# Attention and a feed-forward block on one core: probabilities copied by transfers and transposed as float32r, with another order of the work in a slot

## The chip, the core and the metric

The kernel runs on one core of one Trainium2 chip. The metric is the device time of one execution in microseconds (us). Five engines work side by side, each through its own instructions in the order in which they were written: TensorE (PE in the profile, its weight loads PEld), VectorE (DVE), ScalarE (ACT), GpSimd (POOL) and SyncE (SP), whose queue issues all transfers here. They wait for one another by semaphores.

## The reference, cut to what matters

```python
# q, k, v: 8 batches x 8 heads x 576 x 64; f: 8 x 8 x 576
scores = q @ k.T / 8 + (cum[:, None] - cum[None, :])     # cum = cumsum(log(clip(f)))
scores = where(causal, -1e9, scores)
attn = softmax(scores)                                   # row maximum taken off, sum + 1e-9
x = heads of (attn @ v) side by side                     # 8 x 576 x 512
xn = (x - mean(x)) / sqrt(var(x) + 1e-6) * g_ln
out = x + relu(xn @ w_ch1) @ w_ch2                       # 512 -> 2048 -> 512
```

The precision wanted is that of float32. TensorE multiplies float32r operands quicker than float32 ones but with fewer bits, so most operands are kept as a high part (float32r) and a low part (the rest, float32r too), and a product is made of two or three matmuls.

## The kernel before, in words

There are 64 heads (n). A head's 576 queries are cut into tiles of 64, 128, 128, 128 and 128 rows (t = 0 to 4), and tile t needs only the keys up to its own. The work is a row of *slots*, one for each head and t = 1 to 4; t = 0 rides along with t = 1. Heads 0 to 15 ("full") work in float32 while the weights are being prepared; heads 16 to 63, the *later heads*, work with high and low parts.

In a slot, pieces named by letters are recorded in the order that a string of ORDERS gives. From slot 66 on (the later heads but for the first two slots and a bit) one string holds to the end. The pieces:

- Q: scores of this slot's tile, `s` (lines L373 and L374: two matmuls, from `hi` and from `kl` and `xq`). S: mask and row maximum on VectorE, from `s` into the softmax tile `p` (L406). e: exponential and row sum on ScalarE, in place (L417). B: reciprocal of the sum on VectorE (L422, L423), normalisation on GpSimd (L424).
- t: transposes on TensorE, `tr` from `p`, of the tile of two slots ago (LAG = 2), 128 columns at a time (L430): 3, 3, 4 and 5 of them for t = 1 to 4. h: ScalarE copies `tr` into the high part `ph` (L486). l: VectorE writes the low parts into `ph` and `pl` (L491).
- A: probabilities times values, `o` from `ph`, `pl` and `vv` (L525), in the slots t = 1 and t = 3, each for two tiles, the later of which was transposed in the slot before. F and a: the result goes by way of `ot` into `xs` (L561, L572) and from there to memory.
- M: the first feed-forward matmul, twelve of 256 columns into `h` (L604 to L606). r: ScalarE makes its high part (L612). m: VectorE makes the low part (L617). N: the second one for the step before, six of 512 columns into `acc` (L626 to L628).
- R: loads (`xr`) and splitting (`x`) of tokens for the next chunk of 256 tokens; near a chunk's end the chunk's rows are loaded (`xw`) and, two slots later, transposed (`xp`, L430 too), copied by ScalarE (`xt`, L651) and their mean and variance taken by VectorE (`bs`, L656). After a chunk's last N two VectorE instructions (L685) form the output. A chunk takes 16 feed-forward steps, one a slot: four heads.
- P: preparation of the next head: ScalarE casts `raw` into `hi` (L339 in slot t = 2, L345 in t = 3), GpSimd makes the low parts, VectorE `xq` and `vv`; also the load of `raw` for the head after that. L: a few small GpSimd instructions.

All tiles come from pools with a fixed number of buffers (`p` has three), so that a write waits for the last reader of its buffer. The transposes take `p` as float32 with `ident`, the identity's float32 view.

Of the kernel before, what the change touches and what calls it, by code (L numbers as in the profile page):

```python
# [8 lines left out]
F32 = mybir.dt.float32  # L9
F32R = mybir.dt.float32r  # L10
# [16 lines left out]
NFULL = 16  # L27
# [20 lines left out]

ORDERS = [
    (0, "WwQsSthAeMrgFBmlLNPaRf"),  # L50
    (37, "WwQSstAMhPelgNFrfmBLRa"),
    (66, "AthQFlMSPNreamRBL"),
]


# [1 line left out]
def attn_moe(ctx: ExitStack, tc: tile.TileContext, qk, v, f, g, w1, w2, out):  # L57
    nc = tc.nc

    const = ctx.enter_context(tc.tile_pool(name="const", bufs=1))  # L60
    work = ctx.enter_context(tc.tile_pool(name="work", bufs=1))
# [5 lines left out]
    pools = {}  # L67
# [14 lines left out]
    ident = identr.bitcast(F32)  # L82

    def busy(n):
# [9 lines left out]
        out=mask[:, S - P :], in_=mask[:, S - P :], pattern=[[-1, P]], base=0,  # L94
# [42 lines left out]
    class WPrep:  # L137
# [131 lines left out]
        late = None  # L269
# [32 lines left out]
    def new_xq(name, dt):  # L302
        xq = work.tile([66, S], dt, tag="xq", bufs=2, name=name)
        nc.gpsimd.memset(xq[64:66, :].bitcast(F32), 1.0)
        return xq

    def load(n):
        h = Head()
        h.n, h.full = n, n < NFULL
        if h.full:  # L310
            h.kl = work.tile([66, S], F32, tag="kl", bufs=2, name=f"kl{n}")
            if len(xfs) < 2:
                xfs.append(new_xq(f"xf{n}", F32))
            h.xq = xfs[n % 2]
            nc.sync.dma_start(out=h.xq[0:64, :], in_=qk[n][0:64, 0, :])
            nc.sync.dma_start(out=h.kl[0:64, :], in_=qk[n][0:64, 1, :])
            if n > 0:
                nc.sync.dma_start(out=h.kl[64:66, :], in_=cumd[n])
        else:
            h.raw = pools["late"].tile([P, 2, S], F32, tag="raw", bufs=1, name=f"raw{n}")  # L320
            nc.sync.dma_start(out=h.raw, in_=qk[n])
# [9 lines left out]
    def prep_a(h):  # L331
        n = h.n
        h.hi = pools["late"].tile([P, 2, S], F32R, tag="hi", bufs=2, name=f"hi{n}")
        h.kl = work.tile([66, S], F32R, tag="kl", bufs=2, name=f"kl{n}")
        if len(xqs) < 2:
            xqs.append(new_xq(f"xq{len(xqs)}", F32R))
        h.xq = xqs[(n - NFULL) % 2]
        nc.sync.dma_start(out=h.kl[64:66, :].bitcast(F32), in_=cumd[n])
        nc.scalar.copy(out=h.hi[:, 1, :], in_=h.raw[:, 1, :])  # L339
        nc.gpsimd.tensor_tensor(  # L340
            out=h.kl[0:64, :], in0=h.raw[0:64, 1, :], in1=h.hi[0:64, 1, :].bitcast(F32), op=ALU.subtract
        )

    def prep_b(h):
        nc.scalar.copy(out=h.hi[:, 0, :], in_=h.raw[:, 0, :])  # L345
        nc.vector.tensor_copy(out=h.xq[0:64, :], in_=h.raw[0:64, 0, :])
        nc.gpsimd.tensor_tensor(
            out=h.hi[64:128, 0, :], in0=h.raw[64:128, 0, :], in1=h.hi[64:128, 0, :].bitcast(F32), op=ALU.subtract
        )

    def prep_v(h):
# [24 lines left out]
                z, sp = a + QT[0][2], sp[: QT[0][1], : QT[0][2]]  # L376
            h.s[t].append((a, z, sp))

    corners, padded = [], {}

    def padded_keys(tag, width, zeros):
        if tag not in padded:
# [36 lines left out]
    def softmax_b(h, t):  # L419
        q0, m, w = QT[t]  # L420
        pt, st = h.p[t]
        nc.vector.tensor_scalar_add(st[:m, 3:4], st[:m, 2:3], 1e-9)  # L422
        nc.vector.reciprocal(st[:m, 3:4], st[:m, 3:4])  # L423
        nc.gpsimd.tensor_scalar(  # L424
            out=pt[:m, :w], in0=pt[:m, :w], scalar1=st[:m, 3:4], scalar2=1.0, op0=ALU.mult, op1=ALU.mult
        )

    def tr(out_, in_):
        m = in_.shape[0]
        nc.tensor.transpose(out_, in_, ident[:m, :m])  # L430

# [196 lines left out]
    def tokens(c, k, t0, m, out_):  # L630

        t = t0
        while t < t0 + m:
            b, o = divmod(t, S)
            src, o0, lim = (xd1[b], 0, S1) if o < S1 else (xd2[b], S1, S)
            w = min(t0 + m - t, lim - o)
            nc.sync.dma_start(out=out_[:, t - t0 : t - t0 + w], in_=src[P * k : P * k + P, o - o0 : o - o0 + w])
            t += w

    def rows_load(c, i):  # L640
        c.xw = m2(f"xw{c.n}_{i}", F32).rearrange("p (k c) -> p k c", k=KT)
        for k in range(KT):
            tokens(c, k, c.n * C + P * i, P, c.xw[:, k, :])

    def chunk_rows(c, i):

# [128 lines left out]
    for u, slot in enumerate(slots):  # L775

        def before(k):
            return slots[u - k] if u >= k else None

        if slot is not None:  # L780
            n, t = slot
            h = hd[n]
        av = None
        if before(LAG + 1) is not None and before(LAG + 1)[1] in (2, 4):
            av = hd[before(LAG + 1)[0]]
        want = moe.can(wp.ready()) and u >= FIRST_MOE

        def piece(c):
            tu = before(LAG)
            if c == "t" and tu is not None:  # L790
                transpose_unit(hd[tu[0]], tu[1])
            elif c == "h" and tu is not None:
                transposed_hi(hd[tu[0]], tu[1])
            elif c == "l" and tu is not None:
                transposed_lo(hd[tu[0]])
            elif c == "Q" and slot is not None:
                if t == 1:
                    qk_mm(h, 0)
                qk_mm(h, t)
            elif c == "A" and av is not None:  # L800
                av_unit(av, before(LAG + 1)[1])
            elif c == "S" and slot is not None:
                if t == 1:
                    softmax_a(h, 0)
                softmax_a(h, t)
            elif c == "e" and slot is not None:
                if t == 1:
                    softmax_e(h, 0)
                softmax_e(h, t)
            elif c in FILL:  # L810
                wp.fill(FILL[c])
            elif c == "s":
                wp.sums()
                if u == LAG:
                    busy(WARM[2])
            elif c == "F" and av is not None:
                finish(av)
            elif c == "a" and av is not None:
                finish_add(av)
            elif c == "r" and want:  # L820
                moe.first_high()
            elif c == "R":
                moe.limit = min(NCHUNK, max(0, u - LAG - 1) // (4 * H) * S // C)
                moe.rest()
            elif c == "L":
                run_later(RSTD)
            elif c == "M" and want:
                moe.first()
            elif c == "B" and slot is not None:
                if t == 1:  # L830
                    softmax_b(h, 0)
                softmax_b(h, t)
            elif c == "m" and want:
                moe.first_low()
            elif c == "W":
                due = 1 + min(u, W_CHANGE) / W_SLOTS + max(0, u - W_CHANGE) * W_TICKS
                while not wp.done() and wp.tick_no <= due:
                    wp.tick()
            elif c == "N":
                moe.second()  # L840
            elif c == "P":
                prep()

        def prep():

            if slot is not None:
                if t == 1 and n + 1 < NFULL:
                    start_head(n + 1)
                if n == NFULL - 2 and t == 1:
                    while not wp.done():  # L850
                        wp.tick()
                        wp.fill(99)
                    early.close()
                    pools["late"] = ctx.enter_context(tc.tile_pool(name="late", bufs=1))
                if n + 1 >= NFULL and n + 1 < B * H:
                    if t == 2:
                        prep_a(hd[n + 1])
                    if t == 3:
                        prep_b(hd[n + 1])
                if t == 3 and n + 2 >= NFULL and n + 2 < B * H:  # L860
                    start_head(n + 2)
                if not h.full and t == LAG + 1:
                    prep_v(h)
                if t == LAG + 1 and n + 1 < B * H:
                    load_v(hd[n + 1])

        for c in [o for first, o in ORDERS if first <= u][-1]:
            piece(c)
# [47 lines left out]
```

## Time and profile before

| | |
|---|---|
| median of 3 runs (lowest to highest) | 1228.06 us (1227.03 to 1229.16) |
| the profiled execution's own time | 1236.05 us |
| its span in the profile | 1234.3 us |
| busy share of the span: PE, PEld, DVE, ACT, POOL | 98%, 88%, 62%, 52%, 36% |
| transfers | 98.82 MB in q1, 26.5% of 16 engines |

In the profile a row of a timeline gives start, duration, engine, line, operation, output and inputs, and in square brackets the idle time before it and what ended that. A row by form gives the count, the busy time, the mean duration in ns of one, and the idle time before. Matmuls are pipelined, so that their records overlap: what one costs is read from the starts of neighbours. In a window's row the width comes first, then the busy time of PE, PEld, DVE, ACT and POOL with their counts, the granted clock of TensorE, the transfers' share and GB/s.

### The profile page before, as it was taken

Reading aid. Unit: us, or ns where it says so; the run is one execution under the profiler, and the core shown is the slowest. Engines: PE = TensorE matmul, PEld = TensorE weight load, DVE = VectorE, ACT = ScalarE, POOL = GpSimd, SP = SyncE. Lnnn points to the kernel's source line nnn. Section 1 sums busy time; section 2 is a strip of 40 time slices with the busy share of each in tenths; the row PEclk is TensorE's granted clock in tenths of the full one; section 3 lists DMA queues with packets and bytes.
Section 4 is the critical chain, followed back from the end, with each engine's and each line's share of the span. In section 5 each row is a group of like instructions: output and inputs, shape, how many; then the busy total and the mean of one; then the engine's idle time right before and its main releaser. Section 6 shows DMA issues by size and latency. Waiting matters only on the chain.

```text
span 1234.3 us, 25357 instructions
## 1 busy us (share of the span) xinstructions
PE 1210.6 (98%) x8368; PEld 1088.0 (88%) x8368; DVE 762.5 (62%) x2664; ACT 643.4 (52%) x1936; POOL 445.1 (36%) x767
## 2 busy tenths in 40 slices
PE   8888998999999999999999999999999999999998
PEld 6666887899999999999999999999999999999997
DVE  6777684477776767777767676767777762222222
ACT  5887574555655555555555555556555542112111
POOL 3444343444444435343434344444444320000000
PEclk8998998999999999999999999999999999999999
DMA  6454351222223232322222222222222311110100
GB/s 174 138 169 143 117 157 57 76 68 79 81 77 94 77 94 77 89 78 84 71 73 90 81 90 81 73 89 82 79 64 76 95 37 36 51 35 26 44 26 27
DMA packets 91253, 100.45 MB, mean 81 GB/s; under 512 B 26865, under 2 KB 76017, under 8 KB 91121
## 3 DMA queue, kind: packets, MB, share of 16 engines
q1 hardware_dynamic: 91120, 98.82, 26.5%
q8 instruction: 67, 1.10, 0.4%
q14 instruction: 66, 0.53, 0.1%
HBM read 79.61 MB, written 19.17 MB: 80 GB/s over the span
## 4 chain that ended last, share of the span: by engine, by line
PE 93%; DVE 3%; ACT 2%; DMA 1%; POOL 1%; issue 1%; DVEq 0%; SPq 0%; ACTq 0%; POOLq 0%
PE h L604 11%; PE h L605 11%; PE h L606 11%; PE acc L626 11%; PE acc L627 11%; PE acc L628 11%; PE tr L430 8%; PE o L525 6%; PE s L373 3%; PE s L374 3%; PE s L371 3%; PE o L500 2%; PE xp L430 1%; PE pc L201 1%; DVE p L406 1%; ACT p L417 1%
## 5 line engine op out<-in xcount | busy, mean ns | idle before, releaser
L424 POOL TENSOR_SCALAR p<-p,st 64x64 f32<-64x64 f32 (+4 forms) x320 | 168.9, 532 | 454.6 <-DVE st L423 161.2
L604 PE MATMUL h<-x,w1h 128*128 128x256 f32 x1152 | 329.3, 286 | 0.4 <-DVE st L406 0.4
L605 PE MATMUL h<-x,w1h 128*128 128x256 f32 x1152 | 325.4, 282 | 0.0
L606 PE MATMUL h<-x,w1l 128*128 128x256 f32 x1152 | 325.4, 282 | 0.0
L612 ACT ACTIVATE hh<-h 128x256 fp32r<-128x256 f32 x288 | 110.7, 384 | 308.7 <-PE h L606 308.4
L617 DVE SCALAR_TENSOR_TENSOR hh<-h,hh 128x256 fp32r<-128x256 f32 x288 | 121.1, 420 | 186.0 <-ACT hh L612 179.8
L626 PE MATMUL acc<-w2h,hh 128*128 128x512 f32 x576 | 228.2, 396 | 0.0
L627 PE MATMUL acc<-w2l,hh 128*128 128x512 f32 x576 | 227.6, 395 | 0.0
L628 PE MATMUL acc<-w2h,hh 128*128 128x512 f32 x576 | 224.7, 390 | 0.0
L604 PEld LDWEIGHTS h<-x,w1h 128*128 128x128 f32 x1152 | 219.2, 190 | 6.1 <-issue 0.9
L605 PEld LDWEIGHTS h<-x,w1h 128*128 128x128 f32 x1152 | 219.7, 191 | 3.3
L606 PEld LDWEIGHTS h<-x,w1l 128*128 128x128 f32 x1152 | 219.4, 190 | 0.0
L417 ACT ACTIVATE p<-p,st 64x64 f32<-64x64 f32 (+4 forms) x320 | 178.3, 558 | 60.3 <-DVE st L406 58.4
L486 ACT CAST ph<-tr 64x128 fp32r<-64x128 f32 (+4 forms) x384 | 109.2, 333 | 124.6 <-PE tr L430 107.1
L430 PE MATMUL tr<-identr,p 128*128 128x128 f32 (+1 forms) x896 | 143.1, 276 | 8.9 <-POOL p L424 6.8
L430 PEld LDWEIGHTS tr<-identr,p 128*128 128x128 f32 (+1 forms) x896 | 101.0, 131 | 38.9 <-POOL p L424 18.2
L406 DVE CUSTOM_DVE_ANT_0 p<-s,mask 64x64 f32<-64x64 f32 (+4 forms) x320 | 130.2, 419 | 7.1 <-PE s L371 3.5
L628 PEld LDWEIGHTS acc<-w2h,hh 128*128 128x128 f32 x576 | 108.3, 188 | 24.8
L491 DVE TENSOR_TENSOR ph<-tr,ph 64x192 fp32r<-64x192 f32 x192 | 57.8, 301 | 115.2 <-ACT ph L486 112.3
L626 PEld LDWEIGHTS acc<-w2h,hh 128*128 128x128 f32 x576 | 109.4, 190 | 14.1 <-issue 0.2
L627 PEld LDWEIGHTS acc<-w2l,hh 128*128 128x128 f32 x576 | 109.3, 190 | 11.8
L373 PE MATMUL s<-hi 128*128 128x288 f32 (+4 forms) x288 | 96.2, 355 | 0.0
(84 smaller groups left out, 1828.0 us busy)
## 6 DMA issues: line engine op xcount, KB each, us to landing
raw<-in_qk_dram SPq DMA_DIRECT2D x48, 576.0 KB
wr<-in_w_dram SPq DMA_DIRECT2D x32, 512.0 KB
vr<-in_v_dram SPq DMA_DIRECT2D x64, 160.0 KB
out_dram<-xt SPq DMA_DIRECT2D x36, 256.0 KB
xa<-xs SPq DMA_DIRECT2D x32, 160.0 KB
xb<-xs SPq DMA_DIRECT2D x32, 128.0 KB
xw<-xa SPq DMA_DIRECT2D x64, 64.0 KB
xw<-xb SPq DMA_DIRECT2D x48, 64.0 KB
```

The lines of the kernel that those rows point to most:

```text
L373: mm(sp, h.hi[:, 0, q0 : q0 + m], h.hi[:, 1, a:z], start=True, stop=False)
L406: nc.vector.tensor_tensor_reduce(out=pt[:m, a:z], in0=sp, in1=mask[:m, off + a : off + z], scale=-SCALE, scalar=3.0e38 if i == 0 else st[: ...
L417: nc.scalar.activation(pt[:m, :w], pt[:m, :w], AF.Exp, bias=st[:m, i : i + 1], scale=-1.0, accum_out=st[:m, 2:3])
L424: nc.gpsimd.tensor_scalar(out=pt[:m, :w], in0=pt[:m, :w], scalar1=st[:m, 3:4], scalar2=1.0, op0=ALU.mult, op1=ALU.mult)
L430: nc.tensor.transpose(out_, in_, ident[:m, :m])
L604: mm(ph, w1h[:, k, fs], c.x[k][:, 0, :], start=(k == 0), stop=False)
L605: mm(ph, w1h[:, k, fs], c.x[k][:, 1, :], start=False, stop=False)
L606: mm(ph, w1l[:, k, fs], c.x[k][:, 0, :], start=False, stop=(k == KT - 1))
L617: nc.vector.scalar_tensor_tensor(out=h[:, 1, :], in0=ph, scalar=0.0, in1=h[:, 0, :].bitcast(F32), op0=ALU.max, op1=ALU.subtract)
L626: mm(c.acc[i], h[:, 0, ts_], w2h[:, j, :], start=(j == 0), stop=False)
L627: mm(c.acc[i], h[:, 0, ts_], w2l[:, j, :], start=False, stop=False)
L628: mm(c.acc[i], h[:, 1, ts_], w2h[:, j, :], start=False, stop=(j == FT - 1))
```

## The change

For later heads, piece B issues one more thing: a transfer copies the normalised `p` into a tile `pw` of type float32r (for t = 0 a small one, `pw0`, made once; for even t a tile of its own with one buffer; for odd t one of the three buffers of `p`). The transposes read `pw` with the identity as float32r and write their output as float32r. The chunk's rows `xw` are loaded into a float32r tile too, by the same transfers as before, and transposed as such. `raw` becomes two tiles, one for the keys and one for the queries, each with a load of its own, in a new piece D at the end of the slots t = 2 and t = 3. And the string for the slots from 66 on is another.

```diff
 ORDERS = [
     (0, "WwQsSthAeMrgFBmlLNPaRf"),
-    (37, "WwQSstAMhPelgNFrfmBLRa"),
-    (66, "AthQFlMSPNreamRBL"),
+    (37, "WwQSstAMhPelgNFrfmBDLRa"),
+    (66, "QSAFeMaBPrthNmlRLD"),
 ]
...
+    def load_raw(h, i):
+        h.raw[i] = pools["late"].tile([P, S], F32, tag=f"raw{i}", bufs=1, name=f"raw{h.n}_{i}")
+        nc.sync.dma_start(out=h.raw[i], in_=qk[h.n][:, i, :])
...
         nc.gpsimd.tensor_scalar(
             out=pt[:m, :w], in0=pt[:m, :w], scalar1=st[:m, 3:4], scalar2=1.0, op0=ALU.mult, op1=ALU.mult
         )
+        if not h.full:
+            if t == 0:
+                if not words:
+                    words.append(pools["late"].tile([P, D], F32R, tag="pw0", bufs=1, name="pw0"))
+                    nc.gpsimd.memset(words[0].bitcast(F32), 0.0)
+                pw = words[0]
+            elif t % 2 == 0:
+                pw = pools["late"].tile([P, S], F32R, tag="pw", bufs=1, name=f"pw{h.n}_{t}")
+            else:
+                pw = work.tile([P, S], F32R, tag="p", bufs=3, name=f"pw{h.n}_{t}")
+            nc.sync.dma_start(out=pw[:m, :w].bitcast(F32), in_=pt[:m, :w])
+            h.p[t] = (pw, st)

     def tr(out_, in_):
         m = in_.shape[0]
-        nc.tensor.transpose(out_, in_, ident[:m, :m])
+        if in_.dtype == F32R:
+            nc.tensor.transpose(out_.bitcast(F32R), in_, identr[:m, :m])
+        else:
+            nc.tensor.transpose(out_, in_, ident[:m, :m])
...
     def rows_load(c, i):
-        c.xw = m2(f"xw{c.n}_{i}", F32).rearrange("p (k c) -> p k c", k=KT)
+        c.xw = m2(f"xw{c.n}_{i}", F32R).rearrange("p (k c) -> p k c", k=KT)
         for k in range(KT):
-            tokens(c, k, c.n * C + P * i, P, c.xw[:, k, :])
+            tokens(c, k, c.n * C + P * i, P, c.xw[:, k, :].bitcast(F32))
```

How the instructions stand then. TensorE, head 49, slot t = 1 (names carry the head, the tile and a buffer number); before:

```order
L525 MATMUL o48_2_10776<-ph1_48_10673,vv48_10709 128x320
L525 MATMUL o48_2_10776<-ph1_48_10673,vv48_10709 128x256
L525 MATMUL o48_2_10776<-ph1_48_10673,vv48_10709 128x128
L525 MATMUL o48_2_10776<-pl1_48_10674,vv48_10709 64x256
L525 MATMUL o48_2_10776<-pl1_48_10674,vv48_10709 64x128
L430 MATMUL tr48_3_10784<-identr_71,p48_3_10701 64x128
L430 MATMUL tr48_3_10784<-identr_71,p48_3_10701 128x128 x3
L373 MATMUL s49_0_0_10791<-hi49_10645 64x128
L374 MATMUL s49_0_0_10791<-kl49_10646,xq1_2930 64x128
L373 MATMUL s49_1_0_10794<-hi49_10645 128x192
L374 MATMUL s49_1_0_10794<-kl49_10646,xq1_2930 128x192
L604 MATMUL h9_8_10802<-x9_0_9876,w1h_135 128x256
```

and after:

```order
L376 MATMUL s49_0_0_11145<-hi49_10999 64x128
L377 MATMUL s49_0_0_11145<-kl49_11000,xq1_2939 64x128
L376 MATMUL s49_1_0_11148<-hi49_10999 128x192
L377 MATMUL s49_1_0_11148<-kl49_11000,xq1_2939 128x192
L543 MATMUL o48_2_11156<-ph1_48_11077,vv48_11070 128x320
L543 MATMUL o48_2_11156<-ph1_48_11077,vv48_11070 128x256
L543 MATMUL o48_2_11156<-ph1_48_11077,vv48_11070 128x128
L543 MATMUL o48_2_11156<-pl1_48_11078,vv48_11070 64x256
L543 MATMUL o48_2_11156<-pl1_48_11078,vv48_11070 64x128
L622 MATMUL h9_8_11167<-x9_0_10210,w1h_135 128x256
```

The scores moved ahead of A, and the transposes behind M's twelve matmuls: `tr48_3` now stands between the last L624 and the first L644 (N), and reads `pw48_3`.

VectorE from slot t = 3 to t = 4 of head 49, where a chunk's rows are transposed in t = 3 (`bs`, `sv` are their statistics, `st` the softmax sums, ISA is S); before:

```order
L617 SCALAR_TENSOR_TENSOR hh9_10_10963<-h9_10_10931,hh9_10_10963 128x256
L656 BN_STATS bs9_0_10977<-xt9_0_10973 128x6
L657 BN_AGGR sv9_10975<-bs9_0_10977 128x2
L422 TENSOR_SCALAR st49_3_10945<-st49_3_10945 128x1
L423 RECIPROCAL st49_3_10945<-st49_3_10945 128x1
L491 TENSOR_TENSOR ph1_49_10915<-tr49_2_10991,ph1_49_10915 64x128
L491 TENSOR_TENSOR pl1_49_10916<-tr49_2_10991,ph1_49_10915 128x256
L406 ISA p49_4_11018,st49_4_11019<-s49_4_0_10997,mask_129 128x288
L406 ISA st49_4_11019 128x1
```

and after:

```order
L674 BN_STATS bs9_0_11356<-xt9_0_11352 128x6
L675 BN_AGGR sv9_11354<-bs9_0_11356 128x2
L409 ISA p49_4_11375,st49_4_11376<-s49_4_0_11369,mask_129 128x288
L409 ISA st49_4_11376 128x1
L409 ISA p49_4_11375,st49_4_11376<-s49_4_1_11372,mask_129,st49_4_11376 128x288
L409 ISA st49_4_11376 128x1
L425 TENSOR_SCALAR st49_4_11376<-st49_4_11376 128x1
L426 RECIPROCAL st49_4_11376<-st49_4_11376 128x1
L635 SCALAR_TENSOR_TENSOR hh9_11_11398<-h9_11_11380,hh9_11_11398 128x256
L509 TENSOR_TENSOR ph1_49_11330<-tr49_2_11400,ph1_49_11330 64x128
L509 TENSOR_TENSOR pl1_49_11331<-tr49_2_11400,ph1_49_11330 128x256
```

Before, the low part of `tr49_2` came ahead of the slot's S; now S, the sums and m stand between the statistics and that low part, which A reads in the next slot. ScalarE at the same place, after (L420 is e, L630 r, L504 h, L669 the copy of the chunk's rows):

```order
L669 COPY xt9_0_11352<-xp9_0_11347 128x512
L420 ACTIVATE p49_4_11375,st49_4_11376<-p49_4_11375,st49_4_11376 128x576
L630 ACTIVATE hh9_11_11398<-h9_11_11380 128x256
L504 CAST ph1_49_11330<-tr49_2_11400 64x128
L504 CAST ph1_49_11330<-tr49_2_11400 128x256
```

Before, h of `tr49_2` stood right behind the copy `xt9_0`, and r and e behind it.

VectorE at a chunk's end, from slot t = 1 to t = 2 of head 51; before:

```order
L685 SCALAR_TENSOR_TENSOR xt9_1_11096<-acc9_1_10427,rs9_10976,xt9_1_11096 128x512
L572 TENSOR_TENSOR xs50_0_11308<-o50_2_11287,ot50_0_11309 64x320
L617 SCALAR_TENSOR_TENSOR hh10_0_11341<-h10_0_11313,hh10_0_11341 128x256
L422 TENSOR_SCALAR st51_0_11326<-st51_0_11326 64x1
L423 RECIPROCAL st51_0_11326<-st51_0_11326 64x1
L422 TENSOR_SCALAR st51_1_11329<-st51_1_11329 128x1
L423 RECIPROCAL st51_1_11329<-st51_1_11329 128x1
L491 TENSOR_TENSOR ph2_50_11293<-tr50_4_11353,ph2_50_11293 64x128
```

and after:

```order
L703 SCALAR_TENSOR_TENSOR xt9_1_11485<-acc9_1_10782,rs9_11355,xt9_1_11485 128x512
L635 SCALAR_TENSOR_TENSOR hh10_0_11723<-h10_0_11700,hh10_0_11723 128x256
L509 TENSOR_TENSOR ph2_50_11725<-tr50_3_11727,ph2_50_11725 64x128
L509 TENSOR_TENSOR pl2_50_11726<-tr50_3_11727,ph2_50_11725 128x3x128
L409 ISA p51_2_11750,st51_2_11751<-s51_2_0_11747,mask_129 128x320
L409 ISA st51_2_11751 128x1
L425 TENSOR_SCALAR st51_2_11751<-st51_2_11751 128x1
L426 RECIPROCAL st51_2_11751<-st51_2_11751 128x1
L635 SCALAR_TENSOR_TENSOR hh10_1_11777<-h10_1_11754,hh10_1_11777 128x256
L509 TENSOR_TENSOR ph2_50_11725<-tr50_4_11779,ph2_50_11725 64x128
```

The low part of `tr50_4`, wanted by A in slot t = 3, moved from right behind the chunk's end to behind two low parts more, S, the sums and the next m.

More of the change, by code (lines that the diff above doesn't have):

```diff
@@ L319, in load @@
         else:
-            h.raw = pools["late"].tile([P, 2, S], F32, tag="raw", bufs=1, name=f"raw{n}")
-            nc.sync.dma_start(out=h.raw, in_=qk[n])
-        return h
+            h.raw = {}
+        return h
+    def load_raw(h, i):
+        h.raw[i] = pools["late"].tile([P, S], F32, tag=f"raw{i}", bufs=1, name=f"raw{h.n}_{i}")
+        nc.sync.dma_start(out=h.raw[i], in_=qk[h.n][:, i, :])
     def load_v(h):
@@ L338, in prep_a @@
         nc.sync.dma_start(out=h.kl[64:66, :].bitcast(F32), in_=cumd[n])
-        nc.scalar.copy(out=h.hi[:, 1, :], in_=h.raw[:, 1, :])
+        nc.scalar.copy(out=h.hi[:, 1, :], in_=h.raw[1])
         nc.gpsimd.tensor_tensor(
-            out=h.kl[0:64, :], in0=h.raw[0:64, 1, :], in1=h.hi[0:64, 1, :].bitcast(F32), op=ALU.subtract
+            out=h.kl[0:64, :], in0=h.raw[1][0:64, :], in1=h.hi[0:64, 1, :].bitcast(F32), op=ALU.subtract
         )
     def prep_b(h):
-        nc.scalar.copy(out=h.hi[:, 0, :], in_=h.raw[:, 0, :])
-        nc.vector.tensor_copy(out=h.xq[0:64, :], in_=h.raw[0:64, 0, :])
+        nc.scalar.copy(out=h.hi[:, 0, :], in_=h.raw[0])
+        nc.vector.tensor_copy(out=h.xq[0:64, :], in_=h.raw[0][0:64, :])
         nc.gpsimd.tensor_tensor(
-            out=h.hi[64:128, 0, :], in0=h.raw[64:128, 0, :], in1=h.hi[64:128, 0, :].bitcast(F32), op=ALU.subtract
+            out=h.hi[64:128, 0, :], in0=h.raw[0][64:128, :], in1=h.hi[64:128, 0, :].bitcast(F32), op=ALU.subtract
         )
@@ L377, in qk_mm @@
             h.s[t].append((a, z, sp))
-    corners, padded = [], {}
+    corners, padded, words = [], {}, []
     def padded_keys(tag, width, zeros):
@@ L842, in piece, with next_raw @@
                 prep()
+            elif c == "D":
+                next_raw()
+        def next_raw():
+            if slot is not None and t in (2, 3) and NFULL <= n + 2 < B * H:
+                if t == 2:
+                    start_head(n + 2)
+                load_raw(hd[n + 2], 1 if t == 2 else 0)
         def prep():
@@ L859, in prep @@
                         prep_b(hd[n + 1])
-                if t == 3 and n + 2 >= NFULL and n + 2 < B * H:
-                    start_head(n + 2)
                 if not h.full and t == LAG + 1:
```

## The prediction

> **What bounds the kernel now.** I read the page's head, then the later heads' stretch as a window, then the waits of TensorE there.
>
> ```profile
> span 1234.3 us, 25357 instructions
> PE 1210.6 (98%) x8368; PEld 1088.0 (88%) x8368; DVE 762.5 (62%) x2664; ACT 643.4 (52%) x1936; POOL 445.1 (36%) x767
> ```
> ```profile
> 250.00:1000.00 750.00, 749.87 (x5313) 693.79 (x5312) 537.48 (x1919) 434.60 (x1315) 327.13 (x538) 1.00 0.26 81
> ```
> ```profile
> PEld xp L430 <- issue: 0.3, 1, 0.3
> ```
>
> From 250 to 1000 us TensorE (first number behind the width) is busy 749.87 of 750 us at full granted clock (1.00), and its waits are one of 0.3 us. So this stretch lasts as long as its matmuls follow one another; what shortens or holds TensorE's row there moves the end, nothing else does. The profiled execution took 1236.05 us (span 1234.3 and 1.75 around it), 8 us over the median of the runs, 1228.06; I work out a difference and put it on the median.
>
> **What an instruction costs in TensorE's row** is read from the starts of neighbours (records overlap, so durations say nothing):
>
> ```profile
> 501.31 0.28 PE L604 MATMUL h<-x,w1h 128*128 128x256 f32 x1
> ...
> 502.74 0.40 PE L626 MATMUL acc<-w2h,hh 128*128 128x512 f32 x1
> ...
> 504.13 0.49 PE L525 MATMUL o<-ph,vv 128*128 128x320 f32 x3
> 504.45 0.34 PE L525 MATMUL o<-pl,vv 128*64 128x256 f32 x2
> 504.62 0.60 PE L430 MATMUL tr<-identr,p 128*64 128x128 f32 x4
> ...
> 505.12 0.23 PE L374 MATMUL s<-kl,xq 66*64 66x128 f32 x1
> 505.18 0.31 PE L373 MATMUL s<-hi 128*128 128x192 f32 x1
> 505.33 0.27 PE L374 MATMUL s<-kl,xq 66*128 66x192 f32 x1
> 505.44 0.30 PE L604 MATMUL h<-x,w1h 128*128 128x256 f32 x1
> ```
> ```profile
> 508.28 0.60 PE L430 MATMUL tr<-identr,p 128*64 128x128 f32 x4
> 508.71 0.27 PE L430 MATMUL tr_4b<-identr,p 128*128 128x128 f32 x1
> ```
> ```profile
> L430 PEld LDWEIGHTS tr<-identr,p 128*128 128x128 f32 x576 | 72.2, 142 | 11.9 <-issue 1.3
> L430 PEld LDWEIGHTS tr<-identr,p 128*64 128x64 f32 x320 | 33.0, 112 | 27.1 <-POOL p L424 18.2 <-issue 4.2 <-POOL kl L340 0.3
> L373 PEld LDWEIGHTS s<-hi 128*128 128x128 f32 x240 | 45.6, 190 | 0.0
> L373 PEld LDWEIGHTS s<-hi 128*64 128x64 f32 x48 | 6.6, 137 | 0.0
> ```
>
> - Four float32 transposes (508.28 to 508.71) take 0.108 each, for 128 moving columns.
> - A float32r matmul of 128 moving columns takes 0.06 (505.12 to 505.18). 320+256+128 columns take 0.32 (504.13 to 504.45): 0.455 ns a column.
> - 192 columns should so take 0.087, but 505.33 to 505.44 is 0.11: there the load of the next 128 weight columns sets the pace. Two loads of `hi` differ by 53 ns for 64 columns, so 128 take about 0.107. The float32 transposes' loads differ by only 30 ns for 64.
> - M (12 matmuls, 501.31 to 502.74) takes 1.43, N (six, to 504.13) 1.39.
>
> **The change, part by part.**
>
> *Transposes as float32r.* No row shows one. From below: nothing gained, 0.108, if load or array go as before. From above: 0.06, the float32r matmul's. I take 0.06: 0.108 is two passes of 128 columns at 0.455 ns, the float32r matmul needs one, and the load in transpose mode is already the faster of the two. A gain of 0.048 counts only between transposes of a group: the last is followed by an ordinary load of 128 columns, which needs 0.11 anyway. Groups of 3, 3, 4 and 5 a head leave 11 gaps, 48 later heads 528; the tokens' 36 groups of four (`xp`) 108. 636 x 0.048 = 30.5 us less.
>
> *The new order on TensorE* removes no instruction. But A, which ended before a 64-column transpose (its last 128 moving columns cost 0.06), now ends before M's 128-column load: 0.11. Twice a head, 96 x 0.05 = 4.8 us more. Q then stands behind N's 512 columns, which hide its load.
>
> *The copies.* 240 copies p to pw and 48 more loads (raw split in two) go through SP's queue. An issue there takes 0.33, so six more a head are 2.0 us, on a queue that computes nothing.
>
> ```profile
> 516.87 0.33 SPq L321 DMA_DIRECT2D raw<-in_qk_dram  x1
> ```
> ```profile
> 88.59 3.36 DMA kl<-in_qk_dram
> ```
> ```profile
> 9.45 4.88 DMA wr<-in_w_dram
> ```
>
> Each copy waits for GpSimd's normalisation; behind it in SP's queue wait raw (read four slots later), xr and xw (one and two slots later) and vr. The largest copy has 288 KB, between kl's 144 KB (3.36 us) and wr's 512 KB (4.88). It is issued some 0.7 us into the slot after its own, and its transpose stands behind Q and M of the slot after that: an estimate of 5.1 us, from the slots' lengths worked out below. I take the lower row (both ends of a copy are on the core) and cost it at nothing; the cover is that slot between. The Trainium skill (DMA: Bandwidth & Descriptors, "Anatomy of one DMA") gives 2.0 us plus bytes over 436e3 on GpSimd's path, an estimate of 2.7 us here; no row shows such a copy, and the sum doesn't use it. The copies' 38.5 MB over 750 us are 51 GB/s beside 81 at a share of 0.26. Softmax tiles `p` come free two slots later than their copy's issue, also covered.
>
> *Transposes late in the slot.* Here is the price. What A multiplies (`ph`, `pl`) was made a slot earlier, with M, N and more between; now a group t in slot t=2 or t=4 is followed only by N (1.39) and the next Q before A needs it. And on ScalarE h stands behind r, behind the casts of P, behind e, which waits for S on VectorE; S stands behind everything VectorE still has of the slot before. Durations and hand-offs:
>
> ```profile
> 524.71 0.60 PE L430 MATMUL xp<-identr,xw 128*128 128x128 f32 x4
> ...
> 525.40 0.59 ACT L651 COPY xt<-xp 128x512 f32<-128x512 f32 x1 [0.73 <-PE xp L430]
> ...
> 526.02 0.69 DVE L656 BATCH_NORM_STATS2 bs<-xt 128x6 f32<-128x512 f32 x1 [1.42 <-ACT xt L651]
> ...
> 526.57 0.68 ACT L339 CAST hi<-raw 128x576 fp32r<-128x576 f32 x1
> 526.75 0.18 DVE L657 BATCH_NORM_AGGREGATE sv<-bs 128x2 f32<-128x6 f32 x1
> ...
> 527.43 0.28 DVE L491 TENSOR_TENSOR ph<-tr,ph 64x128 fp32r<-64x128 f32 x1
> 527.69 0.39 ACT L612 ACTIVATE hh<-h 128x256 fp32r<-128x256 f32 x1 [0.44 <-PE h L606]
> 527.75 0.56 DVE L491 TENSOR_TENSOR pl<-tr,ph 128x384 fp32r<-128x384 f32 x1
> 528.22 0.28 DVE L491 TENSOR_TENSOR pl<-tr_4b,ph 128x128 fp32r<-128x128 f32 x1
> 528.42 0.48 DVE L406 CUSTOM_DVE_ANT_0 p<-s,mask 128x320 f32<-128x320 f32 x1
> 528.82 0.42 DVE L617 SCALAR_TENSOR_TENSOR hh<-h,hh 128x256 fp32r<-128x256 f32 x1
> 528.94 0.56 ACT L417 ACTIVATE p<-p,st 128x320 f32<-128x320 f32 x1 [0.86 <-DVE st L406]
> ```
> ```profile
> 535.06 0.45 DVE L406 CUSTOM_DVE_ANT_0 p<-s,mask 128x288 f32<-128x288 f32 x1
> 535.66 0.52 DVE L406 CUSTOM_DVE_ANT_0 p<-s,mask,st 128x288 f32<-128x288 f32 x1
> 536.28 0.78 ACT L417 ACTIVATE p<-p,st 128x576 f32<-128x576 f32 x1
> 536.97 0.19 ACT L417 ACTIVATION_READ_ACCUMULATOR p<-p,st 128x1 f32 x1
> ```
> ```profile
> L685 DVE SCALAR_TENSOR_TENSOR xt<-acc,rs,xt 128x512 f32<-128x512 f32 x36 | 25.4, 746 | 12.4 <-PE acc L628 12.4
> ```
>
> Neighbours on ScalarE and VectorE overlap by about 0.1 (527.75 to 528.22 for 0.56); a hand-off takes 0.03 (xt's end to bs). I count from the start of the slot in which the late t stands.
>
> TensorE: from the start of slot t=2 to A in t=3: Q 640 columns 0.29, M 1.43, t 4 x 0.06 + 0.11, N 1.39, Q 896 columns 0.41: A at 3.87. From t=4: Q 1152 columns 0.53, M 1.43, t 0.23, N 1.39, next head's Q 0.38 (505.18 to 505.44 and two of 0.06): A at 3.96.
>
> An ordinary slot t=2: S can start at 0.5, l is done 2.7 later (the chain below) at 3.2: 0.67 spare. Slot t=4: 0.45 spare by the same chain. So ordinary slots don't stall. Three do, once in four heads (a chunk of tokens):
>
> - xp in slot t=1. The last xp is at -0.11; xt 0.31 behind (0.36 in the rows, less the shorter stream), at 0.20; bs at 0.82; S at 1.65 (behind the aggregate). Then e +0.52, the cast hi +0.56, r +0.58, r's end +0.39, m +0.03, l +0.34, its end +0.28: 4.35. TensorE waits from 3.87, with the hand-off: 0.53.
> - The chunk's end in slot t=1: xt of the output (0.75 each) waits for N's second half, 0.25 to 1.0; m 0.92, l of the group before 1.26 and 1.58, S at 2.05, 0.40 later than above: 0.93.
> - xp in slot t=3: S at 1.65, second half +0.60, e +0.62, r +0.78, its end +0.39, m +0.03, l +0.34, end +0.28: 4.69 against 3.96: 0.78.
>
> Together 2.24 a chunk; chunks 1 to 12 fall under the new order: 26.9 us more.
>
> **Sum:** -30.5 + 4.8 + 26.9 = +1.2 us: 1237.3 for the profiled execution, 1229 on the median. Where the gain goes: into TensorE's waits for VectorE before A. An error of 0.2 in each of 36 waits is 7 us, so this case's own range is 1222 to 1236.
>
> **Rivals.**
>
> - *The waits before A don't come up* (each chain 0.5 to 0.9 shorter than I count, say because hand-offs overlap more). Then only TensorE's row counts: -25.7, 1202. For it: VectorE is busy 537 of 750 us, ScalarE 435, and a group that slips a little costs nothing before 0.45 of spare is gone. Against: each link is a measured row, in program order. Half the waits give 1216.
> - *The float32r transposes run no faster*, since the load sets the pace: the change then doesn't do what it says. For it: 505.33 to 505.44. Then one gap a head (64 columns to 64) gains, 2.3; 4.8 is lost; slots grow by 0.19 (t=2) and 0.10 (t=4), so waits shrink to 2.24 - 0.48 = 1.76 a chunk, 21 us. +23.6: 1252, slower. It decides from a load of 0.107 on; against it stands the transposes' 30 ns for 64 columns, which makes 0.06 for 128. The Trainium skill (TensorE: Matmul & The Clock Gate, "LDWEIGHTS") has a load cost its columns over 1.2 GHz, 107 ns for 128, which is this rival; the trace agrees on `hi` and not on the transposes.
> - *The copy lands too late.* From 5.1 us on each head waits at t; 0.5 us beyond that costs 48 x 0.5 = 24 us, 1253. For it: wr's 4.88. Against: kl's 3.36.
>
> **How the numbers follow.** My case 0.42, no waits 0.22, about half the waits 0.14, transposes no faster 0.15, copy too late 0.07. This kernel's runs tell 0.2% (2.5 us) from nothing: 1225.6 to 1230.5 is "same". Faster: 0.22 + 0.14 + a quarter of my case 0.10 = 0.46. Same: a third of my case, 0.14. Slower: the rest of it 0.18 + 0.22 = 0.40. The range 1201 to 1247 leaves out the upper part of the last two cases (0.15) and a little below 1201.
>
> **What would show it.** Starts of neighbouring tr matmuls 0.06 apart (0.11: the second rival). Waits of TensorE at o for VectorE's ph, about 36 in number, 0.5 to 0.9 each, behind xp and behind the output's xt; none would be the first rival. Waits at tr for a transfer would be the third. A head without one of the three slots would be 0.43 us shorter (11 x 0.048 less 2 x 0.05).

## The result: 3.1% slower

The changed kernel takes 1268.65 us (median; 1265.45 to 1271.99), the kernel before 1228.61 us beside it: a ratio of 1.0314 (95% interval [1.0262, 1.0366]). The prediction was 1229 us with a range from 1201 to 1247.

The first row of the chain that ended last, before; then, after, the busy shares, the same row of the chain, and the later heads' stretch as a window:

```profile
PE 93%; DVE 3%; ACT 2%; DMA 1%; POOL 1%; issue 1%; DVEq 0%; SPq 0%; ACTq 0%; POOLq 0%
```
```profile
PE 1208.8 (96%) x8368; PEld 1076.5 (85%) x8368; DVE 755.6 (60%) x2664; ACT 621.9 (49%) x1936; POOL 445.6 (35%) x768
PE 67%; DVE 13%; ACT 9%; issue 4%; DMA 4%; SPq 2%; POOL 1%; DVEq 0%; POOLq 0%; ACTq 0%
250.00:1000.00 750.00, 718.08 (x5059) 655.41 (x5058) 505.83 (x1831) 396.15 (x1258) 311.58 (x507) 1.00 0.40 125
```

TensorE, busy 749.87 of these 750 us before, now stands for 32 of them, at the same granted clock (1.00). VectorE and ScalarE, 5% of the chain that ended last before, are 22% of it now. The waits of TensorE, and of ScalarE at the splitting of tokens, from 260 to 1030 us (total, times, longest):

```profile
PE o L543 <- DVE ph L509: 28.6, 36, 2.4
ACT x L606 <- DMA xr<-xb: 14.4, 7, 4.6
ACT x L606 <- DMA xr<-xa: 12.1, 8, 3.1
```

TensorE waits nearly always in one place, at `o` (A), for VectorE's `ph`: 36 times in this stretch, 39 in the whole run. The prediction had 36, but the stretch is shorter than its twelve chunks, and some of the waits belong to longer chunks that it did not have. The waits of ScalarE for `xr` are new: the prediction had none.

The output's two VectorE instructions come once a chunk, so their starts are a clock for chunks of four heads. Before (L685), the first and last of the twelve chunks under the new order, and one chunk between; then the same after (L703), with a second, longer chunk:

```profile
213.64 0.75 DVE L685 SCALAR_TENSOR_TENSOR xt<-acc,rs,xt 128x512 f32<-128x512 f32 x1 [3.17 <-PE acc L628]
...
735.81 0.75 DVE L685 SCALAR_TENSOR_TENSOR xt<-acc,rs,xt 128x512 f32<-128x512 f32 x1 [0.66 <-PE acc L628]
...
800.74 0.75 DVE L685 SCALAR_TENSOR_TENSOR xt<-acc,rs,xt 128x512 f32<-128x512 f32 x1 [0.67 <-PE acc L628]
...
995.52 0.75 DVE L685 SCALAR_TENSOR_TENSOR xt<-acc,rs,xt 128x512 f32<-128x512 f32 x1 [0.67 <-PE acc L628]
```
```profile
206.84 0.75 DVE L703 SCALAR_TENSOR_TENSOR xt<-acc,rs,xt 128x512 f32<-128x512 f32 x1 [3.17 <-PE acc L646]
...
278.48 0.75 DVE L703 SCALAR_TENSOR_TENSOR xt<-acc,rs,xt 128x512 f32<-128x512 f32 x1 [0.98 <-PE acc L646]
...
348.27 0.75 DVE L703 SCALAR_TENSOR_TENSOR xt<-acc,rs,xt 128x512 f32<-128x512 f32 x1 [0.98 <-PE acc L646]
...
751.87 0.75 DVE L703 SCALAR_TENSOR_TENSOR xt<-acc,rs,xt 128x512 f32<-128x512 f32 x1 [0.98 <-PE acc L646]
...
818.74 0.75 DVE L703 SCALAR_TENSOR_TENSOR xt<-acc,rs,xt 128x512 f32<-128x512 f32 x1 [0.98 <-PE acc L646]
...
1026.25 0.75 DVE L703 SCALAR_TENSOR_TENSOR xt<-acc,rs,xt 128x512 f32<-128x512 f32 x1 [0.98 <-PE acc L646]
```

Twelve chunks took 781.9 us before and 819.4 after: 37.5 more, nearly all of the 40 between the medians. (The profiled executions differ by only 31, because the one before was 8 us over its median; at its first row here it was already 7 us later than the one after.) The 37.5 have two layers. A regular chunk went from 64.9 to 66.9: 2.0 x 12 = 24. Seven chunks are longer still, such as 278.48 to 348.27 (69.8): another 14 together. (The first is one of them. It was 2.5 longer than the others before too, and only what goes beyond that is counted.)

In a regular chunk three of the 16 slots hold a wait of TensorE before A, 1.17, 0.88 and 0.70 us over the same slot elsewhere. The first, at the chunk's end, on VectorE:

```profile
550.82 1.41 DVE L703 SCALAR_TENSOR_TENSOR xt<-acc,rs,xt 128x512 f32<-128x512 f32 x2 [0.98 <-PE acc L646]
552.15 0.42 DVE L635 SCALAR_TENSOR_TENSOR hh<-h,hh 128x256 fp32r<-128x256 f32 x1
552.60 0.28 DVE L509 TENSOR_TENSOR ph<-tr,ph 64x128 fp32r<-64x128 f32 x1
...
553.37 0.48 DVE L409 CUSTOM_DVE_ANT_0 p<-s,mask 128x320 f32<-128x320 f32 x1
...
555.42 0.42 DVE L635 SCALAR_TENSOR_TENSOR hh<-h,hh 128x256 fp32r<-128x256 f32 x1 [0.49 <-ACT hh L630]
555.95 0.28 DVE L509 TENSOR_TENSOR ph<-tr,ph 64x128 fp32r<-64x128 f32 x1
```

and on ScalarE and TensorE:

```profile
553.89 0.56 ACT L420 ACTIVATE p<-p,st 128x320 f32<-128x320 f32 x1 [3.28 <-DVE st L409]
...
554.46 0.66 ACT L342 CAST hi<-raw 128x576 fp32r<-128x576 f32 x1
555.02 0.37 ACT L630 ACTIVATE hh<-h 128x256 fp32r<-128x256 f32 x1
555.29 0.62 ACT L504 CAST ph<-tr 64x128 fp32r<-64x128 f32 x2
```
```profile
551.23 0.31 PE L376 MATMUL s<-hi 128*128 128x320 f32 x1
551.38 0.31 PE L377 MATMUL s<-kl,xq 66*128 66x320 f32 x1
...
555.02 0.37 PE L377 MATMUL s<-kl,xq 66*128 66x448 f32 x1
556.28 0.80 PE L543 MATMUL o<-ph,vv 128*128 128x256 f32 x5 [0.89 <-DVE ph L509]
```

The matmuls of S's scores start at 551.23 and 551.38; S starts at 553.37, behind the output, m and l of the slot before. ScalarE has stood 3.28 us for it, then runs e, the cast, r and h without a pause, and `ph` is done at 556.23 (555.95 and 0.28), when TensorE has been ready for a microsecond.

### The profile page after: what moved, and what is told of

Read it like the earlier page. It is cut to its first block, busy times and chain, and to the rows that moved or that the text cites. A ratio compares the mean times of both kernels' runs of the same rounds, so it can differ in the third digit from the quotient of the medians.

```text
span 1264.8 us, 26082 instructions
## 1 busy us (share of the span) xinstructions
PE 1208.8 (96%) x8368; PEld 1076.5 (85%) x8368; DVE 755.6 (60%) x2664; ACT 621.9 (49%) x1936; POOL 445.6 (35%) x768
## 4 chain that ended last, share of the span: by engine, by line
PE 67%; DVE 13%; ACT 9%; issue 4%; DMA 4%; SPq 2%; POOL 1%; DVEq 0%; POOLq 0%; ACTq 0%
PE h L622 9%; PE acc L644 8%; PE h L623 8%; PE h L624 8%; PE acc L645 8%; PE acc L646 8%; PE o L543 5%; ACT p L420 4%; DVE p L409 4%; PE tr L446 2%; PE s L374 2%; DMA pw<-p 2%; PE o L518 2%; PE s L376 2%; PE s L377 2%
## 5 line engine op out<-in xcount | busy, mean ns | idle before, releaser
L427 POOL TENSOR_SCALAR p<-p,st 64x64 f32<-64x64 f32 (+4 forms) x320 | 173.7, 544 | 542.0 <-ACT p L420 193.4
L624 PE MATMUL h<-x,w1l 128*128 128x256 f32 x1152 | 326.4, 283 | 0.0
L420 ACT ACTIVATE p<-p,st 64x64 f32<-64x64 f32 (+4 forms) x320 | 179.1, 560 | 211.4 <-DVE st L409 209.2
L644 PE MATMUL acc<-w2h,hh 128*128 128x512 f32 x576 | 242.2, 420 | 0.0
L646 PE MATMUL acc<-w2h,hh 128*128 128x512 f32 x576 | 226.6, 393 | 0.0
L624 PEld LDWEIGHTS h<-x,w1l 128*128 128x128 f32 x1152 | 221.0, 192 | 0.0
L630 ACT ACTIVATE hh<-h 128x256 fp32r<-128x256 f32 x288 | 109.1, 379 | 181.7 <-PE h L624 178.2
L409 DVE CUSTOM_DVE_ANT_0 p<-s,mask 64x64 f32<-64x64 f32 (+4 forms) x320 | 133.1, 424 | 19.2 <-PE s L377 5.6
L425 DVE TENSOR_SCALAR st<-st 128x1 f32<-128x1 f32 (+1 forms) x320 | 47.8, 149 | 122.0 <-ACT p L420 118.3
L644 PEld LDWEIGHTS acc<-w2h,hh 128*128 128x128 f32 x576 | 108.6, 189 | 13.7 <-ACT ph_full L504 0.2
L504 ACT CAST ph<-tr 64x128 fp32r<-64x128 f32 (+4 forms) x384 | 107.2, 329 | 0.2
L579 ACT COPY ot<-o 64x320 f32<-64x320 f32 x96 | 38.0, 396 | 129.5 <-PE o L543 129.2
L543 PEld LDWEIGHTS o<-ph,vv 128*128 128x128 f32 x384 | 54.4, 188 | 44.2 <-DVE ph L509 26.9
L543 PE MATMUL o<-ph,vv 128*128 128x256 f32 (+2 forms) x384 | 61.4, 281 | 31.0 <-DVE ph L509 31.0
```

Source lines behind the costliest of these rows:

```text
L409: nc.vector.tensor_tensor_reduce(out=pt[:m, a:z], in0=sp, in1=mask[:m, off + a : off + z], scale=-SCALE, scalar=3.0e38 if i == 0 else st[: ...
L420: nc.scalar.activation(pt[:m, :w], pt[:m, :w], AF.Exp, bias=st[:m, i : i + 1], scale=-1.0, accum_out=st[:m, 2:3])
L427: nc.gpsimd.tensor_scalar(out=pt[:m, :w], in0=pt[:m, :w], scalar1=st[:m, 3:4], scalar2=1.0, op0=ALU.mult, op1=ALU.mult)
L543: mm(o, st, mv, start=first, stop=True, skip_group_check=True)
L624: mm(ph, w1l[:, k, fs], c.x[k][:, 0, :], start=False, stop=(k == KT - 1))
L630: nc.scalar.activation(h[:, 0, :], c.ph, AF.Relu)
```

## The experiments

Line numbers in these kernels differ from the changed kernel's by up to some 20. A "chunk" is the distance between two output rows. Each ratio is to the kernel before as measured beside that run.

**The waits behind VectorE.** Statistics and output instructions (and what follows the statistics on GpSimd, the chunk's factors) are set aside and recorded behind the next slot's S:

```diff
         bs = work.tile([P, 6], F32, tag="bs", bufs=2, name=f"bs{c.n}_{i}")
-        nc.vector.bn_stats(bs, xt)
-        nc.vector.bn_aggr(c.sv[:, i, :], bs)
+        def stats():
+            nc.vector.bn_stats(bs, xt)
+            nc.vector.bn_aggr(c.sv[:, i, :], bs)
+        put_off(stats)
...
-                    chunk_out(c)
+                    put_off(lambda: chunk_out(c))
...
                 softmax_a(h, t)
+                run_behind_s()
```

> The changed kernel, with a chunk's statistics (bs, sv) and its two output instructions on VectorE recorded behind the next slot's S instead of ahead of it. Theory one (the waits before A come from VectorE: S stands behind bs or behind the output's xt, and so e, r, m and l come late): the three waits of a chunk, 1.17, 0.88 and 0.70 us over a plain slot in the changed kernel's trace, go. 2.75 x 12 = 33 us less: about 1235 us. Rival (the waits come from ScalarE, where xt's copy from xp stands ahead of e, or from the longer way of t past M): they stay, at least the two behind xp (1.58 x 12 = 19), and no more than 14 us is gained: 1254 or above.

Measured: 1240.66 us, ratio to before 1.0084 [1.0051, 1.0117]; 28 us under the changed kernel. Chunks that wait for nothing else are as long as this one:

```profile
738.20 0.75 DVE L721 SCALAR_TENSOR_TENSOR xt<-acc,rs,xt 128x512 f32<-128x512 f32 x1
...
802.30 0.75 DVE L721 SCALAR_TENSOR_TENSOR xt<-acc,rs,xt 128x512 f32<-128x512 f32 x1
```

64.1 us, all three waits gone: 66.9 - 64.1 = 2.8 a chunk, 33 for twelve. `xt`'s copy on ScalarE stayed where it was, so the theory holds and the rival falls. The waits of ScalarE for `xr` remain, and in the shorter slots the copies themselves begin to come late:

```profile
PE tr L446 <- DMA pw<-p: 5.2, 5, 1.8
```

This wait of TensorE was 0.3 us in the changed kernel. VectorE's S, too, now waits for copies out of a buffer of `p` that it is to write (6 waits, 15.7 us; none in the changed kernel), which the prediction had as covered. So the twelve chunks together give 23 us, not 33 (819.4 to 796.1): the chunks made longer by `xr` stay, and are longer by more. The medians differ by 28.

With the output alone put off:

> The changed kernel with only the output's two VectorE instructions behind the next slot's S; the statistics stay ahead of it. Theory (each wait belongs to its own piece of VectorE's work): the wait at the chunk's end (1.17 us over a plain slot) goes, those behind xp (0.88 and 0.70) stay: 12 x 1.17 = 14 us less, about 1254 us, chunks of 65.7 where nothing waits for xr. Rival (what counts is VectorE's load of a chunk, so that any relief spreads): all three shrink.

Measured: 1256.57 us, 1.0211 [1.0184, 1.0238]; a regular chunk 65.7 us, its two waits behind `xp` as before (0.88 and 0.70). Each wait belongs to its own piece of work.

**The loads behind the copies.** What SP's queue did in a long chunk (rows left out are issues of `xw`), and the instruction of ScalarE that waited for it:

```profile
310.46 1.12 SPq L440 DMA_DIRECT2D pw<-p  x2
311.63 0.58 SPq L655 DMA_DIRECT2D xw<-xb  x1
...
315.59 0.43 SPq L655 DMA_DIRECT2D xr<-xa  x1
316.06 0.43 SPq L655 DMA_DIRECT2D xr<-xb  x1
```
```profile
319.60 0.41 ACT L606 CAST x<-xr 128x256 fp32r<-128x256 f32 x1 [4.62 <-DMA xr<-xb]
```

ScalarE came to x at 314.98, before the load of `xr` was even issued, and e, r and h of the next slot stood behind it. In this chunk `xw` and `xr` come from two tensors (`xa` and `xb`), so that their issues, 0.47 us apart, are twice as many: eight `xw` stand behind two copies, and `xr` behind those. Without the copies (below) the same loads of `xr` are issued at 311.93 and 312.40, although the slots lie 0.6 us later there, and x waits for nothing. What holds the queue (its own waits, 260 to 1030 us):

```profile
SPq L440 <- POOL p L427: 222.8, 155, 3.0
...
SPq L440 <- PE tr_4b L446: 50.2, 34, 2.6
```

The copies (L440) wait for GpSimd's `p` and for the transposes that free a `pw` (`tr_4b` is the last of five). Such a total says little alone: before, the queue waited 311 us for VectorE at the load of `raw` (260 to 1000 us), and TensorE lost nothing by it. What counts is which load stands behind. The experiment splits the first two `xr` of a chunk one slot later:

```diff
-                if len(c.x) < min(old, room):
+                if len(c.x) < min(old - (0 if left == 0 or self.cur is None else 1), room):
```

> The changed kernel, with the first two splits of a chunk's tokens (x from xr) one slot later than before, so that a load of xr has a whole slot more. Theory (the seven chunks that take 0.4 to 4.5 us over the others, 14 us together, do so because SP's queue, held by the copies until GpSimd's p is ready, issues xr late and ScalarE waits at x for it): ScalarE's waits at x for xr, 30 us, go, and 10 to 14 us of time with them: about 1255 us. Rival (these chunks are longer for another transfer, xw, raw or vr, or because pw lands late): the waits at x go, but the time moves by under 4 us.

Measured: 1254.16 us, 1.0189 [1.0162, 1.0217]: 14.5 less. ScalarE has no wait for `xr` left in this stretch, and all chunks but the first are alike (67.1 to 67.5), the one that took 69.8 too (274.06 to 341.24). The excess of the long chunks is gone; a regular chunk is 0.3 longer than it was, so that the twelve together give 11 us (819.4 to 808.1).

**What float32r is worth, and what the copies cost.** First the same copies into float32 tiles:

```diff
...
-                pw = pools["late"].tile([P, S], F32R, tag="pw", bufs=1, name=f"pw{h.n}_{t}")
+                pw = pools["late"].tile([P, S], F32, tag="pw", bufs=1, name=f"pw{h.n}_{t}")
...
```

(`pw0` and the tiles for odd t likewise.)

> The changed kernel, with the copies pw kept but in float32 tiles: later heads' transposes read the copies as float32; xp stays float32r. Theory by the prediction's price (11 gaps a head of 0.048): the float32r transposes save 0.53 us a head, so this is 25 us slower, less some of the waits before A that a longer slot shortens (three a chunk by 0.1 to 0.2, 5 us): about 1288 us. Rival by the row of a plain head (transposes and the N behind them take 6.92 us together, as they did before): float32r saves under 0.2 us a head and this is less than 10 us slower, under 1278.

Then no copies at all (the block in softmax_b that makes `pw` is left out):

> The changed kernel's order and loads, without the copies: later heads' transposes read p as float32, as in the kernel before; xp stays float32r. It differs from the kernel with float32 copies in the copies alone, and from the kernel before in the order (and xp). Theory (copies hold SP's queue and make xr late): 10 to 14 us faster than the float32 copies' kernel, and ScalarE's waits at x for xr are gone. Rival (copies cost nothing, as predicted): the two agree within 4 us. In both cases slower than the kernel before by the waits before A, 2.75 x 12 = 33 us less some 5 for the longer slots, and by the boundaries of the new order (0.1 by the prediction, 0.35 us a head if the row of a plain head is right: 5 to 17 us): 1256 to 1273 us.

Measured: 1277.17 us (1.0374 [1.0339, 1.0409]) with float32 copies, 1266.00 us (1.0280 [1.0240, 1.0321]) without. The first is 8.5 us over the changed kernel by the medians and 10.7 over the twelve chunks (830.1): at the rival's bound of 10 and far from the theory's 25. The rival's reason is too strong, though: in slots without a wait float32r saves some 0.08 us, 0.3 a head, and in the three with one it saves nothing, because VectorE sets their end whatever the transposes take. The copies cost 11 us here, and without them ScalarE waits once for `xr`, 0.9 us. A group of five transposes in the changed kernel, and with float32 copies:

```profile
569.98 0.46 PE L446 MATMUL tr<-identr,pw 128*64 128x128 f32 x4
570.27 0.25 PE L446 MATMUL tr_4b<-identr,pw 128*128 128x128 f32 x1
570.36 0.47 PE L644 MATMUL acc<-w2h,hh 128*128 128x512 f32 x1
570.66 0.40 PE L645 MATMUL acc<-w2l,hh 128*128 128x512 f32 x1
```
```profile
573.63 0.60 PE L448 MATMUL tr<-identr,pw 128*64 128x128 f32 x4
574.06 0.27 PE L448 MATMUL tr_4b<-identr,pw 128*128 128x128 f32 x1
574.09 0.48 PE L644 MATMUL acc<-w2h,hh 128*128 128x512 f32 x1
```

Four gaps take 0.29 instead of 0.43, 0.035 less each. But N starts 0.09 behind the last float32r transpose and 0.03 behind the last float32 one: of 0.14, 0.06 is given back. (N's first matmul takes 0.30 in the one and 0.31 in the other, 574.09 to 574.40, against 0.23 between the others: that comes with the place and not with the type.)

**Both repairs together.**

> The changed kernel with both repairs: a chunk's statistics and output instructions on VectorE behind the next slot's S, and the first two splits of tokens one slot later. Theory (the two causes are separate: 2.8 us a chunk of waits behind VectorE, and xr issued late): a chunk takes 64.1 to 64.5 us in every one of the twelve, 1254.2 - 12 x 2.9 = 1219 us, 0.9% under the kernel before. Rival (when one wait goes, another that it hid comes up, such as a pw that lands late): 1228 or above, no faster than the kernel before.

Measured: 1234.14 us, 1.0034 [1.0016, 1.0052]. The rival's outcome, but not for its reason: every chunk has one wait left, 0.98 us in the slot where the later split now stands beside `xt`. On ScalarE:

```profile
774.38 0.59 ACT L671 COPY xt<-xp 128x512 f32<-128x512 f32 x1 [1.01 <-PE xp L446]
774.86 0.41 ACT L608 CAST x<-xr 128x256 fp32r<-128x256 f32 x1
```

So, on top of both repairs, the loads were made a slot earlier, which puts the splits back where the changed kernel has them:

```diff
-                if n >= self.limit or left > 8:
+                if n >= self.limit or left > 9:
```

> As the kernel with both repairs, but with the tokens' loads one slot earlier and the splits where the changed kernel has them (that kernel put the second split beside xt's copy, and its twelve chunks each had one wait of 0.98 us before A in that slot). Theory: this wait goes, chunks take 64.1 us each, 12 us less than with both repairs: 1222 us, 0.5% under the kernel before. Rival (the wait belongs to xp itself and only the absence of other traffic hid it): 65.1 a chunk and 1234 us as before.

Measured: 1225.33 us, 0.9962 [0.9945, 0.9978]: faster than the kernel before, by 0.4%. Most chunks take 64.1 us, and the twelve 777.5 against 781.9 before:

```profile
729.27 0.75 DVE L721 SCALAR_TENSOR_TENSOR xt<-acc,rs,xt 128x512 f32<-128x512 f32 x1
...
793.37 0.75 DVE L721 SCALAR_TENSOR_TENSOR xt<-acc,rs,xt 128x512 f32<-128x512 f32 x1
```

Of the waits before A three are left in that stretch (they stood at 36), in chunks of up to 65.6 us:

```profile
PE o L543 <- DVE ph L509: 2.2, 3, 1.1
```

**The order without copies, repaired.**

> The new order without the copies (float32 transposes from p), with the statistics and output instructions behind the next slot's S. Theory (waits behind VectorE are the order's own, 2.6 us a chunk here: 1.14, 0.87 and 0.61): 12 x 2.6 = 31 us less than without this repair, 1235 us; the rest over the kernel before, 0.4 us a chunk and some in the stretches beside, is the new order's boundaries in TensorE's row. Against the kernel with both repairs and early loads, the copies and float32r transposes are then worth some 13 us. Rival (without copies the waits come from ScalarE, since SP's queue is free here): less than 10 us is gained, 1256 or above.

Measured: 1231.65 us, 1.0030 [1.0013, 1.0046]. The waits go as expected, 34 us by the medians, 29 over the twelve chunks (816.6 to 787.8). A chunk:

```profile
731.56 0.75 DVE L709 SCALAR_TENSOR_TENSOR xt<-acc,rs,xt 128x512 f32<-128x512 f32 x1
...
796.84 0.75 DVE L709 SCALAR_TENSOR_TENSOR xt<-acc,rs,xt 128x512 f32<-128x512 f32 x1
```

65.3 us against 64.1 with copies and float32r: these are worth 1.2 us a chunk, 14 for twelve where nothing waits. The two kernels themselves are less far apart, 10 over the twelve chunks and 6 by the medians, against the expectation's 13: with copies some chunks still wait.

**The copies under the order of before.**

```diff
-    (66, "QSAFeMaBPrthNmlRLD"),
+    (66, "AthQFlMSPNreamRBDL"),
```

> The changed kernel with the order of the kernel before from slot 66 on (transposes first, B near the slot's end; D behind B): the copies and the float32r transposes alone. Theory (the copies, 3.2 us and up to 0.7 of GpSimd and issue ahead of them, have less than the one slot that is left between B's end and t): TensorE waits at tr for pw, some tenths to 1 us in most slots, 48 heads x 4 x 0.5 = 96 us: about 1310 us; so the order is what pays for the copies. Rival (the copies land in time): no waits at tr, and the float32r transposes give 0.31 us a head and 0.13 a chunk: 17 us less, 1213 us.

Measured: 1344.81 us, 1.0937 [1.0904, 1.0970]. That is 35 us over the theory's 1310, and the rival falls. TensorE waits at the transposes:

```profile
PE tr L446 <- DMA pw<-p: 76.3, 68, 4.7
```

The row is for 260 to 1030 us; over its own twelve chunks (895.6 us, 114 more than before) these waits are 85 us. The granted clock was 0.96 there against 1.00 before, and the rest was not taken apart. With t first and B last there is a slot too little between copy and transpose. The late place of t is what pays for the copies, and the waits before A are the price of that place.

**The tokens' rows alone**, in the kernel before (`xw` as float32r, order and probabilities as they were):

> The kernel before with one part of the change alone: the tokens' rows xw loaded into float32r tiles and transposed as such; order, probabilities and loads as before. By the prediction's price, 36 groups x 3 gaps x 0.048: 5.2 us less. By what the changed kernel's trace shows (a slot with xp 0.42 longer than one without, now 0.36): 0.065 x 36 = 2.3 us less. Both theories: no new wait.

Measured: 1225.03 us, 0.9972 [0.9954, 0.9990]: 3.1 us less. The interval (1.2 to 5.7 us less) holds both prices; the traces are nearer the lower one, 2.5 us over the twelve chunks (779.4) and 0.7 behind them. This part alone gives as much as the repaired whole, within the intervals.

## Why the prediction was wrong

Its sum was +1.2 us. Term by term, with what the runs showed:

| term | predicted | shown | from |
|---|---|---|---|
| later heads' transposes as float32r | -25.3 | -14 | chunks of 64.1 and 65.3, with and without |
| tokens' rows as float32r | -5.2 | -3 | rows alone |
| the new order in TensorE's row | +4.8 | +7 | order without copies, repaired: 65.3 less 64.9, and 0.2 a chunk for `xw` |
| waits before A | +26.9 | +33 | a chunk of 66.9 less 64.1 |
| the copies | 0 | +14 | the seven longer chunks, gone with the split one slot later; 11 by leaving the copies out |
| sum | +1.2 | +37 | 37.5 in the trace |

The figures shown are steps on one way from the chunk of 64.9 us to that of 66.9 and the longer ones, so that their sum has to come out. Neither large error explains the miss alone: with the copies at 0 the rest makes +23, 1252 us, and with the predicted gain for the later heads' transposes it makes +26.

- *"I ... cost it at nothing; the cover is that slot between."* This step failed. `pw` did land in time (288 KB in a median of 3.2 us on the page, under the lower row taken; TensorE waited 0.3 us at `tr` for it). But what stands behind a copy in SP's queue was named, `raw`, `xr`, `xw` and `vr`, and given no price. `xr` is read one slot later; the copies held it until ScalarE stood waiting. At 14 us this is as much as the later heads' float32r transposes gained.
- *The gain of a transpose.* A second step failed here: a gain half the size. In a group of five the four gaps shrink from 0.109 to 0.06 for the first two and 0.09 for the last two, 0.07 on the mean and not 0.06 throughout. And "the last is followed by an ordinary load of 128 columns, which needs 0.11 anyway" does not hold for both alike: the float32 group's last one cost 0.03, and the float32r group's costs 0.07 to 0.09, four times a head. The rival "no faster" was wrong too. The Trainium skill (TensorE: Matmul & The Clock Gate, "LDWEIGHTS") has a load cost its columns over 1.2 GHz, an estimate of 107 ns for 128; four transposes in 0.29 us do not agree with it.
- *The waits before A.* Right in place and number, and each 0.1 to 0.25 too small: 2.24 predicted, 2.75 measured a chunk. At the chunk's end S started 2.14 behind the slot's start (2.05 predicted). Most of the rest is the last link: l came 0.53 behind m's start (555.42 to 555.95), not 0.34. Where nothing else holds it, it comes 0.45 behind (552.15 to 552.60), and here it waited for ScalarE's h as well, which ended at 555.91. That ordinary slots don't stall was right.
- *The 0.05 behind A.* Right in size, and one matmul later than said. A's last matmul still costs 0.06, but M's first, behind A, takes 0.17 where its others take 0.12:

```profile
565.01 0.33 PE L622 MATMUL h<-x,w1h 128*128 128x256 f32 x1
565.18 0.28 PE L623 MATMUL h<-x,w1h 128*128 128x256 f32 x1
565.30 0.28 PE L624 MATMUL h<-x,w1l 128*128 128x256 f32 x1
```

Twice a head, that is the predicted 4.8 us. N's first one, behind the transposes, takes 0.30 in their new place (570.36 to 570.66), against 0.23 between the others; but before, Q's first stood behind them and paid as much (0.24 from 508.74 to 508.98 for 320 columns, 0.15 from 551.23 to 551.38 now), so that this only moved. The 2 us left of the row's 7 are not taken apart.

The errors went the same way, and the time lies 22 us over the range. That was drawn from the terms of the sum and its rivals. The rival on the copies was about their own landing; none stood for the loads behind them, and the two rivals that came out at 1252 and 1253 were in large part left out of the range.

## What to carry to other kernels

A transfer put into an in-order queue can be paid for by whatever is queued behind it, so each load behind it needs a time of issue and a time of use, as the transfer itself does. When a producer is moved next to its consumer on the bounding engine, the other engines' rare work, once a chunk here, decides the wait; moving that work behind the next slot's S took back 28 us. And measure the price of a row over its boundaries: what follows the last of a group belongs to the group.

## What the runs showed of the hardware

A float32 transpose of 128 columns lets the next matmul start 0.03 us after its own recorded start, a float32r one 0.07 to 0.09, although inside a group the float32r ones follow one another faster (0.07 against 0.11 on the mean of a group of five). Behind either, the next matmul of 512 columns takes 0.30 to 0.32 instead of 0.23. Copies on the core of 288 KB landed in a median of 3.2 us:

```profile
pw<-p SPq DMA_DIRECT2D x48, 288.0 KB, 3.2
```
